# A work list reordered: three more query/key tiles transposed by DMA instead of on TensorE, and zero matmuls at the head

## The chip, the cores and the metric

The kernel runs on one core of a Trainium2 chip. The time is that of one execution in microseconds (us) of device time; lower is better. Six executions of the kernel before took 180.29 to 180.58 us, with a median of 180.43 us.

## What is computed

Four batches of eight heads attend over 768 positions of 64 numbers each. A query sees the first 8 positions and the last 96 up to itself, with a bias that falls with the distance. The 3072 results of 512 numbers then go through a layer that takes the maximum of three matrix products, and through an output product.

```python
scores = scale * np.matmul(q, k.transpose(0, 1, 3, 2))
is_global = pos[None, :] < int(n_global)           # 8
is_local = (rel >= 0) & (rel < int(n_local))       # 96
scores = np.where(is_global | is_local, scores - slope * dist, -1e9)
a = softmax(scores); x = np.matmul(a, v)           # -> (3072, 512)
h = np.maximum(np.maximum(x @ w1, x @ w2), x @ w3) # 512 -> 768
out = h @ w_out                                    # 768 -> 512
```

## The kernel before

**Tiles.** The 3072 tokens are 24 tiles T of 128; six tiles make a batch, and T % 6 == 0 is a batch's first. The tiles are grouped into seven chunks c for the output layers: tiles 0-3, 4-5, 6-7, 8-11, 12-15, 16-19, 20-23. All work is cut into units, and the string `SCHEDULE` names every unit in the order in which it is issued. There is no planner at run time: each engine runs its own instructions in exactly the order in which the string issues them, and waits in that order. One waiting instruction holds up all that stand behind it on its engine. SP is the queue that starts all loads, all stores but one, and the DMA transposes.

**Units of attention.** `l`, `L` and `v` load. `c` and `C` cast to bf16; the last digit of a unit picks the engine (0 ACT, 1 DVE, 2 POOL, 3 split). Tiles 0-11 come in parts (`l`, `c`, and `x`, which transposes on PE). Tiles 12-23, the "single" tiles, are loaded by `L`, cast by `C T.0`, and transposed by `X` (`u_X`): with the digit 4 by a DMA transpose on SP (L250), else by eight PE transposes into PSUM (L261) and copies to SBUF by ACT and/or DVE (L263-L266). `S T.g` computes the scores of four heads into the PSUM slot `sp0` or `sp1` (L283; with the digit 1 the bias is added first by two matmuls, L275), and ACT takes the exponential (L288). `M` multiplies by the mask on DVE (L307). `A` multiplies by the values (L322, L325), into one of the same two PSUM slots, and DVE normalizes (L331, L332). `T` transposes the result: digit 4 by DMA on SP (L340), else by four PE transposes and a copy (L349, L350). `G` and `V` put the 8 global keys and values into place: `G T` after the scores of T and before those of T+1, `V T` after `A T` and before `A T+1`.

**Units of the output layers.** `F c.f.j` is one of the three products (j) for one of six slices (f) of a chunk: four matmuls into a PSUM tile of the pool `psH`, emptied by ACT for j = 0 (L366) and by DVE for j = 1, 2 (L368, L370). They are 512 columns wide, but 256 for the chunks 1 and 2. `O c.t` is the output product of one tile: six matmuls of 512 columns (L376), a copy (L382), a store (L383). `E` is the last chunk's output. `w`, `o`, `W`, `Q` load and cast the weights.

**Rings.** `psH` has three PSUM tiles, shared by F, O, some of the transposes and the zero matmuls. `psT` has one. `sp0` and `sp1` are one tile each. The output staging ring has four tiles. A DMA's completion semaphore is one of eight, so a DMA is issued only when the one eight before it has landed.

**Zero matmuls.** `u_D(i, n)` issues n matmuls of the tile `zeros` on itself (L436); nothing reads the result.

Of the kernel before, what the change touches and what calls it, by code (L numbers as in the profile page):

```python
# [22 lines left out]


SCHEDULE = """
    K0 K1 K2 K3 K4 K5 l1.0 l1.1 D0.3 c0.0.2 B0.1 B1.1 B2.1 B3.0 K6 B4.1 B5.1 c0.1.1 c1.0.2 x0.0.4 B6.1
    B7.1 x0.1.4 S0.0.1 v0 l2.0 l2.1 K7 S0.1.1 G0.0 S1.0.1 S1.1.0 x1.0.3 c1.1.2 M0.0 M0.1 M1.0 v1 x1.1.4
    C0.1.2 v2 A0.1 G1.2 S2.0.1 M1.1 c2.0.2 x2.0.1 C1.1.1 S2.1.0 G2.2 S3.0.1 M2.0 M2.1 C2.1.1 T0.1 S3.1.1
    M3.0 M3.1 c2.1.2 v3 A1.0 C3.1.0 w0.0 V1.2 x2.1.2 w1.0 A2.1 V2.2 A3.0 T1.0 T2.1 T3.1 W1.0.1 W0.0.0
    G3.2 S4.0.0 S4.1.0 F0.0.0 F0.1.0 M4.0 F0.2.0 F0.3.0 G4.1 S5.0.0 M4.1 S5.1.0 w0.1 W0.1.1 w0.2 W0.2.2  # L30
    V3.2 F0.0.1 F0.1.1 F0.0.2 F0.1.2 v4 C4.1.0 A4.0 V4.2 w1.1 W1.1.2 W2.0.0 F0.4.0 F0.5.0 M5.0 M5.1 w1.2
    W1.2.2 v5 W2.1.0 T4.0 F0.2.1 F0.3.1 l3.0 l3.2 F0.4.1 l3.1 c3.0.2 c3.2.2 F0.5.1 o2 C5.1.0 A5.1 l3.3
    F0.2.2 Q2.2 F0.3.2 W2.2.0 o0 T5.0 F0.4.2 o1 F0.5.2 x3.0.0 F1.0.0 F1.1.0 c3.1.1 F1.2.0 x3.2.0 Q0.2
    F1.0.1 F1.1.1 F1.2.1 l4.0 l4.1 c3.3.0 F1.0.2 F1.1.2 F1.2.2 x3.1.2 x3.3.1 F1.3.0 F1.4.0 Q1.2 F1.3.1
    S6.0.0 S6.1.0 v6 v7 v8 G6.0 F1.3.2 F1.5.0 v9 c4.0.1 F1.4.1 S7.0.0 S7.1.0 G7.2 v10 M6.0 M6.1 M7.0
    M7.1 O0.0.0 F1.4.2 c4.1.1 C6.1.2 C7.1.2 L12 F1.5.1 S8.0.0 S8.1.0 x4.0.0 O0.1.0 A6.0 x4.1.2 A7.1 V7.2
    F1.5.2 v11 T6.0 O0.2.0 T7.1 G8.2 C8.1.2 S9.0.0 S9.1.0 G9.1 v12 v13 O0.3.0 F2.0.0 F2.1.0 S10.0.0 M8.0
    M8.1 M9.0 M9.1 S10.1.0 C9.1.2 L13 L14 F2.0.1 F2.1.1 F2.0.2 A8.0 C12.0.1 F2.1.2 G10.2 O1.0.0 V8.2
    A9.1 X12.1 M10.0 M10.1 C10.1.0 C11.1.0 F2.2.0 S11.0.0 S11.1.0 M11.0 M11.1 L15 F2.3.0 F2.4.0 O1.1.0
    V9.2 A10.1 F2.2.1 V10.2 T8.0 F2.3.1 F2.5.0 T9.0 A11.1 F2.4.1 T10.0 F2.2.2 F2.3.2 T11.1 F2.4.2  # L40
    S12.0.0 S12.1.0 F2.5.1 C13.0.2 C14.0.2 C15.0.1 X13.4 F3.0.0 F3.1.0 F3.0.1 G12.1 C12.1.0 F3.2.0
    F3.1.1 F3.2.1 S13.0.0 S13.1.0 F2.5.2 v14 C13.1.0 C14.1.2 M12.0 M12.1 F3.0.2 F3.1.2 X14.4 F3.2.2
    X15.4 G13.2 M13.0 M13.1 S14.0.0 S14.1.0 F3.3.0 F3.4.0 F3.5.0 M14.0 M14.1 G14.1 A12.0 A13.1 F3.3.1
    F3.4.1 F3.5.1 S15.0.0 M15.0 S15.1.0 G15.0 v15 V13.2 L16 L17 v16 T12.4 v17 M15.1 O2.0.0 C15.1.0 A14.0
    V14.2 F3.3.2 F3.4.2 T13.4 F3.5.2 C16.1.0 C16.0.2 X16.3 T14.4 C17.0.2 A15.1 X17.4 O2.1.0 S16.0.0
    S16.1.0 G16.1 L18 V15.2 L19 T15.1 M16.0 O3.0.0 M16.1 F4.0.0 F4.1.0 F4.0.1 F4.1.1 C18.0.2 L20 C19.0.2
    A16.1 F4.2.0 F4.3.0 S17.0.0 S17.1.0 F4.2.1 F4.0.2 F4.3.1 v18 M17.0 v19 M17.1 X18.3 X19.4 C20.0.0
    V16.2 F4.1.2 C17.1.2 O3.1.1 A17.1 F4.2.2 F4.3.2 S18.0.0 M18.0 S18.1.0 M18.1 F4.4.0 T16.4 T17.4
    F4.4.1 C18.1.2 C19.1.1 F4.4.2 X20.4 G18.1 S19.0.0 S19.1.0 F4.5.0 L21 M19.0 M19.1 v20 F4.5.1 A18.0
    T18.4 F4.5.2 A19.1 T19.4 V19.1 C21.0.1 X21.4 G19.1 L22 C22.0.2 L23 X22.4 O3.2.1 O3.3.0 O4.0.1  # L50
    S20.0.0 S20.1.0 M20.0 G20.0 O4.1.0 F5.0.0 F5.1.0 F5.2.0 S21.0.0 S21.1.0 G21.2 F5.0.1 F5.1.1 M20.1
    M21.0 F5.3.0 F5.0.2 F5.1.2 F5.2.1 F5.2.2 v21 C20.1.1 C21.1.2 F5.4.0 S22.0.0 M21.1 S22.1.0 C23.0.0
    F5.3.1 M22.0 M22.1 F5.5.0 F5.3.2 A20.0 V20.2 G22.2 v22 F5.4.1 X23.4 v23 F5.5.1 T20.4 A21.1 V21.1
    T21.4 F5.4.2 F5.5.2 S23.0.0 S23.1.0 M23.0 O4.2.0 M23.1 C22.1.2 A22.0 C23.1.0 O4.3.0 V22.2 T22.4
    A23.1 T23.4 O5.0.1 O5.1.0 O5.2.1 O5.3.0 F6.0.0 F6.1.0 F6.0.1 F6.0.2 F6.2.0 F6.3.0 F6.4.0 F6.1.1
    F6.2.1 F6.1.2 F6.3.1 F6.4.1 F6.2.2 F6.3.2 F6.5.0 F6.4.2 F6.5.1 F6.5.2 E
"""


# [450 lines left out]
```

The softmax here doesn't subtract the row's maximum and nothing guards it: scores larger than these inputs give would overflow.

## Time and profile before

| | |
|---|---|
| median of six executions | 180.43 us |
| the profiled execution | 180.08 us |
| its span, first to last instruction | 178.3 us |
| PE busy (matmul) | 166.4 us, 93% of the span |
| DVE, ACT, POOL busy | 119.2, 103.2, 37.3 us |
| first output-layer matmul (F0.0.0) starts | 23.14 us |
| last copy starts | 175.30 us |

Times inside the execution count from the start of the span. A profile line gives the line of the kernel, the engine, the operation, the output tile, the input tiles and the shape; then the number of instructions, the busy time, the mean time of one, and what ended the idle time before them. PE matmuls are pipelined, so that the time of one (0.38 us for 512 columns) is longer than the slot it takes in a row of them (0.216 us). The chain of waits shows slots.

### The profile page before, as it was taken

The page shows a single profiled execution, that of the slowest core. Times are in us where ns is not written, and L with a number is a line of the kernel's source. Part 1 is how long each engine was busy: PE and PEld are TensorE (multiplying, and loading weights), DVE is VectorE, ACT ScalarE, POOL GpSimd, SP SyncE. Part 2 cuts the span into 40 slices and gives each one's busy share as a digit, 9 for nine tenths or more (in the row PEclk, how much of TensorE's full clock was granted, in tenths as well). Part 3 has the DMA queues.
Part 4 walks back from the last instruction along what each step waited for, and adds up shares of the span by engine and source line. Part 5 has one row for each costly group of instructions (what it writes and reads, how often), then busy time and mean ns, then how long its engine had stood idle before and what let it go on. Part 6 is the DMA issues. An engine that isn't in the chain of part 4 may idle for free.

```text
span 178.3 us, 3963 instructions
## 1 busy us (share of the span) xinstructions
PE 166.4 (93%) x1529; PEld 95.5 (54%) x1551; DVE 119.2 (67%) x237; ACT 103.2 (58%) x160; POOL 37.3 (21%) x65
## 2 busy tenths in 40 slices
PE   3598799999999999999999999999999999999991
PEld 0454645458866677845555555554454555444451
DVE  4629875977796789748978448878357986137610
ACT  4867898737689958555753836351862543440131
POOL 4255203544243012210006024000020401000000
PEclk9999999999999999999999999999999999999999
DMA  5999999999998999799444999669989664700015
GB/s 142 290 271 242 356 321 380 320 360 358 255 204 222 222 250 243 136 206 228 84 90 124 177 252 230 131 123 206 181 158 298 126 129 147 253 12 4 0 46 191
DMA packets 83587, 35.52 MB, mean 199 GB/s; under 512 B 66160, under 2 KB 78320, under 8 KB 83568
## 3 DMA queue, kind: packets, MB, share of 16 engines
q1 hardware_dynamic: 83424, 35.20, 83.3%
q8 instruction: 12, 0.20, 0.5%
q14 instruction: 7, 0.06, 0.1%
q10 hardware_dynamic: 144, 0.07, 0.1%
HBM read 25.17 MB, written 6.29 MB: 176 GB/s over the span
## 4 chain that ended last, share of the span: by engine, by line
PE 83%; SPq 7%; DMA 5%; issue 1%; ACT 1%; DVE 1%; POOL 0%; ACTq 0%
PE h L361 53%; PE po L376 16%; PE sp L283 6%; SPq L158 4%; DMA rawv<-in_v_dram 4%; PE op L322 3%; SPq L174 3%; PE op L325 2%; PE tpp L239 2%; PE xtp L349 2%; DMA out_dram<-ost 1%; ACT ost L382 1%; PE tp L261 1%; DVE xb L332 0%; ACT va L189 0%
## 5 line engine op out<-in xcount | busy, mean ns | idle before, releaser
L361 PE MATMUL h<-xT,w 128*128 128x512 bf16 (+1 forms) x491 | 99.2, 348 | 0.7 <-issue 0.2
L361 PEld LDWEIGHTS <-w 128*128 128x128 bf16 x504 | 47.0, 98 | 40.4 <-DVE w L427 0.3
L288 ACT ACTIVATE P<-sp 128x1024 bf16<-128x1024 f32 (+1 forms) x48 | 43.5, 955 | 20.3 <-PE sp L283 20.0
L368 DVE TENSOR_TENSOR h<-h,h 128x512 bf16<-128x512 bf16 (+1 forms) x42 | 25.3, 609 | 25.6 <-PE h L361 16.3
L366 ACT CAST h<-h 128x512 bf16<-128x512 f32 (+1 forms) x42 | 21.5, 532 | 21.5 <-PE h L361 21.3
L376 PE MATMUL po<-wo,ht 128*128 128x512 bf16 (+2 forms) x147 | 33.1, 362 | 0.5
L370 DVE TENSOR_TENSOR ht<-h,h 128x512 bf16<-128x512 bf16 (+1 forms) x42 | 25.0, 606 | 3.7 <-PE h L361 3.0
L307 DVE TENSOR_TENSOR P<-P,wmask 128x1024 bf16<-128x1024 bf16 x36 | 24.8, 716 | 3.6 <-ACT P L288 3.5
L382 ACT COPY ost<-po 128x512 f32<-128x512 f32 (+2 forms) x20 | 11.2, 564 | 18.4 <-PE po L376 11.2
L376 PEld LDWEIGHTS <-ht 128*128 128x128 bf16 x156 | 14.0, 98 | 13.9
L332 DVE TENSOR_TENSOR xb<-op,rz 128x512 bf16<-128x512 f32 x24 | 16.6, 691 | 0.8
L283 PEld LDWEIGHTS <-qkT 64*128 64x128 bf16 x352 | 10.2, 96 | 9.7 <-issue 8.0
L283 PE MATMUL sp<-qkT 64*128 64x128 bf16 x352 | 15.2, 223 | 0.0
L322 PEld LDWEIGHTS <-P 128*128 128x128 bf16 x192 | 12.5, 97 | 3.0 <-ACT P L288 0.7
L221 POOL COPY va<-vaf 8x260 int32<-8x260 int32 x14 | 6.3, 449 | 34.7 <-PE op L325 34.7
L198 POOL CAST qkb<-raw 128x1024 bf16<-128x1024 f32 x7 | 7.2, 1035 | 27.7 <-DMA raw<-in_k_dram 27.6
L322 PE MATMUL op<-va,P 128*128 128x65 bf16 x160 | 12.4, 193 | 0.5 <-ACT va L189 0.4
L239 PE MATMUL tpp<-identb,qkp 128*128 128x128 bf16 x96 | 7.9, 235 | 4.0 <-POOL qkp L183 3.5
L325 PEld LDWEIGHTS <-P 128*128 128x128 bf16 x160 | 10.5, 97 | 2.0 <-issue 0.4
L325 PE MATMUL op<-va,P 128*128 128x65 bf16 x128 | 9.9, 193 | 0.0
L243 ACT COPY qkT<-tpp 128x1024 bf16<-128x1024 bf16 (+1 forms) x9 | 7.9, 874 | 3.4 <-PE tpp L239 3.4
L239 PEld LDWEIGHTS <-qkp 128*128 128x128 bf16 x96 | 6.4, 106 | 5.8 <-POOL qkp L183 4.4
(66 smaller groups left out, 107.5 us busy)
## 6 DMA issues: line engine op xcount, KB each, us to landing
rawv<-in_v_dram SPq DMA_DIRECT2D x24, 256.0 KB, 5.0
out_dram<-ost SPq DMA_DIRECT2D x23, 256.0 KB, 2.3
rawp<-in_q_dram SPq DMA_DIRECT2D x6, 512.0 KB, 7.3
rawp<-in_k_dram SPq DMA_DIRECT2D x6, 512.0 KB, 7.5
wst<-in_moe_w_dram SPq DMA_DIRECT2D x3, 1024.0 KB, 9.9
raw<-in_q_dram SPq DMA_DIRECT2D x12, 256.0 KB, 4.3
raw<-in_k_dram SPq DMA_DIRECT2D x12, 256.0 KB, 4.8
wst<-in_moe_w_dram SPq DMA_DIRECT2D x3, 512.0 KB, 8.8
```

Of the source, the lines that this page charges most:

```text
L239: nc.tensor.transpose(tp[:, e, j - lo], qb["p", n, s][:, e, 2 * j:2 * j + 2].rearrange("i h d -> i (h d)"), identb)
L283: nc.tensor.matmul(sp[:, hh, j2, ds], qT(T - ds, 1)[hsl, jp], qT(T, 0)[hsl, jp], start=not how, stop=True, skip_group_check=True)
L288: nc.scalar.activation(P[:, :, 0:n], sp.rearrange("p a b d n -> p (a b) d n")[:, :, 0:n], AF.Exp, bias=0.0, scale=scale)
L307: nc.vector.tensor_mul(P, P, wmask[:, g, :, 0:2])
L322: nc.tensor.matmul(o, P[:, i, 0], heads(va[T])[:, h], start=True, stop=(t == 0), skip_group_check=True)
L325: nc.tensor.matmul(o, P[:, i, 1], heads(va[T - 1])[:, h], start=False, stop=True, skip_group_check=True)
L332: nc.vector.tensor_tensor(out=x.rearrange("p (g h) d -> p g h d", g=2), in0=o4[:, :, :, 0:64], in1=rz[:, :, :, None].to_broadcast([128, 2, ...
L361: nc.tensor.matmul(ps, w123[f // 2][:, dm, j, (f % 2) * 128:(f % 2) * 128 + 128], xT[c][:, dm], start=(dm == 0), stop=(dm == 3))
L366: nc.scalar.copy(h01, ps)
L368: nc.vector.tensor_max(h01s[c, f], h01s[c, f], ps)
L370: nc.vector.tensor_max(ht[c][:, f], h01s[c, f], ps)
L376: nc.tensor.matmul(po, ht[c][:, f, tt * 128:(tt + 1) * 128], wo[:, f, cols], start=(f == 0), stop=(f == NF - 1))
```

## The change

The same units are issued in another order, many with another engine digit, and the zero matmuls differ:

- `X`: before, 9 of the 12 single tiles are transposed by DMA, and X12, X16 and X18 on PE. After, all 12 by DMA.
- `T`: 11 by DMA and 13 on PE in both. T8 goes to DMA, T13 to PE.
- `D`: one unit of 3 matmuls of 512 columns before. After, 42 at the head, 12 behind the first transposes and 9 behind the first result, of 128 columns each.
- The value loads v1 and v2 are issued before the second parts of the loads of tiles 4 and 5; the three 512 KB loads of the first weight slices stand together, ahead of the first 1 MB one; the loads of the later tiles stand ahead of more of the output weights. The first weight slices are cast by POOL.
- The engine digits of `c`, `C`, `G`, `V`, `A`, `W`, `O` are dealt anew, some `V` to ACT. The six score units with a bias matmul are the same six.
- The pairs `S T.0 S T.1` are often in the other order or have other units between them; the order of the F units within a chunk is mixed.

The code differs in one line besides the string. The diff, cut:

```diff
 SCHEDULE = """
-    K0 K1 K2 K3 K4 K5 l1.0 l1.1 D0.3 c0.0.2 B0.1 B1.1 B2.1 B3.0 K6 B4.1 B5.1 c0.1.1 c1.0.2 x0.0.4 B6.1
-    B7.1 x0.1.4 S0.0.1 v0 l2.0 l2.1 K7 S0.1.1 G0.0 S1.0.1 S1.1.0 x1.0.3 c1.1.2 M0.0 M0.1 M1.0 v1 x1.1.4
-    C0.1.2 v2 A0.1 G1.2 S2.0.1 M1.1 c2.0.2 x2.0.1 C1.1.1 S2.1.0 G2.2 S3.0.1 M2.0 M2.1 C2.1.1 T0.1 S3.1.1
-    M3.0 M3.1 c2.1.2 v3 A1.0 C3.1.0 w0.0 V1.2 x2.1.2 w1.0 A2.1 V2.2 A3.0 T1.0 T2.1 T3.1 W1.0.1 W0.0.0
-    G3.2 S4.0.0 S4.1.0 F0.0.0 F0.1.0 M4.0 F0.2.0 F0.3.0 G4.1 S5.0.0 M4.1 S5.1.0 w0.1 W0.1.1 w0.2 W0.2.2
...
-    A9.1 X12.1 M10.0 M10.1 C10.1.0 C11.1.0 F2.2.0 S11.0.0 S11.1.0 M11.0 M11.1 L15 F2.3.0 F2.4.0 O1.1.0
...
-    V14.2 F3.3.2 F3.4.2 T13.4 F3.5.2 C16.1.0 C16.0.2 X16.3 T14.4 C17.0.2 A15.1 X17.4 O2.1.0 S16.0.0
...
-    A16.1 F4.2.0 F4.3.0 S17.0.0 S17.1.0 F4.2.1 F4.0.2 F4.3.1 v18 M17.0 v19 M17.1 X18.3 X19.4 C20.0.0
...
-    A23.1 T23.4 O5.0.1 O5.1.0 O5.2.1 O5.3.0 F6.0.0 F6.1.0 F6.0.1 F6.0.2 F6.2.0 F6.3.0 F6.4.0 F6.1.1
+    D2.42 K2 c0.0.0 B3.0 B0.1 B4.1 B2.1 B7.1 B1.1 l1.0 B5.1 B6.1 x0.0.2 K4 c0.1.1 D1.12 K5 x0.1.4 K6
+    S0.0.1 S0.1.1 M0.1 l1.1 S1.0.1 c1.0.1 S1.1.0 K7 c1.1.1 x1.1.4 x1.0.3 M1.0 G0.2 G1.2 v0 C0.1.2 A0.1
+    S2.0.1 M2.0 v1 M1.1 D0.9 S2.1.0 G2.1 S3.0.1 M2.1 C1.1.2 A1.1 V1.0 l2.0 c2.0.2 x2.0.2 K1 v2 C2.1.2
+    A2.0 V2.1 M0.0 l2.1 c2.1.2 v3 w0.0 W0.0.2 S3.1.1 T0.0 C3.1.1 G3.0 M3.0 x2.1.4 A3.0 T1.0 S4.1.0 T2.1
+    T3.1 M3.1 K3 S4.0.0 w0.1 W0.1.2 M4.1 F0.0.0 F0.1.0 F0.1.1 K0 M4.0 w0.2 G4.2 W0.2.2 F0.0.1 w1.0
...
+    T5.0 c3.2.0 F0.5.2 F0.2.2 F1.0.0 F1.5.0 l3.0 c3.0.0 x3.2.0 F1.0.1 F1.0.2 F1.4.0 F1.5.1 F1.5.2 x3.0.0
+    l3.3 F1.2.0 l3.1 c3.3.2 x3.3.2 c3.1.1 x3.1.3 S7.0.0 F0.3.2 M7.0 F1.1.0 S7.1.0 S6.0.0 G6.1 G7.0
+    F1.1.1 F1.1.2 F1.3.0 F1.3.1 l4.0 c4.0.2 v6 C6.1.1 F1.3.2 S6.1.0 M6.1 o0 S8.0.0 o2 v9 C9.1.2 o1
+    x4.0.2 M6.0 F1.4.1 F1.2.1 S8.1.0 A6.0 F1.2.2 Q0.0 F1.4.2 M7.1 F0.4.2 l4.1 Q2.2 c4.1.1 G8.2 S9.0.0
...
+    O1.1.0 T7.1 M8.1 v11 S10.1.0 L14 C8.1.1 S10.0.0 L15 C13.0.2 O0.2.0 C12.0.2 X12.4 M10.1 F2.0.0 F2.5.0
+    A8.0 V8.0 F2.3.0 F2.0.1 F2.3.1 T8.4 A9.0 M10.0 O1.0.1 V9.1 G10.0 F2.3.2 C11.1.1 S11.1.0 M11.1
...
+    M20.0 S20.1.0 F5.5.0 M20.1 F5.5.1 F5.4.0 A20.0 F5.3.0 F5.5.2 G20.2 S21.1.0 M21.1 S21.0.0 G21.1 V20.0
+    F5.4.1 M21.0 F5.3.1 X22.4 S22.1.0 v21 C21.1.2 S22.0.0 M22.1 v23 v22 O4.2.0 A21.1 F5.4.2 V21.2 G22.2
+    S23.0.0 M22.0 S23.1.0 T20.4 T21.4 F5.1.2 C22.1.2 F5.3.2 A22.0 V22.2 M23.1 C23.1.2 O5.0.0 T22.4 M23.0
+    O4.1.0 A23.0 T23.4 O5.2.0 O5.1.1 O5.3.0 F6.0.0 F6.0.1 F6.3.0 F6.2.0 F6.4.0 F6.2.1 F6.2.2 F6.4.1
...
 """
@@ -433,7 +433,7 @@
         wp = psH.tile([128, 512], FP32, name="wp", tag="h")
         for _ in range(n):
-            nc.tensor.matmul(wp, zeros[:, 0:128], zeros, start=True, stop=True)
+            nc.tensor.matmul(wp[:, 0:128], zeros[:, 0:128], zeros[:, 0:128], start=True, stop=True)
```

More of the change, by code (lines that the diff above doesn't have):

```diff
@@ L31 @@
[L31 to L35, printed above, removed]
@@ L36 @@
-    M7.1 O0.0.0 F1.4.2 c4.1.1 C6.1.2 C7.1.2 L12 F1.5.1 S8.0.0 S8.1.0 x4.0.0 O0.1.0 A6.0 x4.1.2 A7.1 V7.2
-    F1.5.2 v11 T6.0 O0.2.0 T7.1 G8.2 C8.1.2 S9.0.0 S9.1.0 G9.1 v12 v13 O0.3.0 F2.0.0 F2.1.0 S10.0.0 M8.0
-    M8.1 M9.0 M9.1 S10.1.0 C9.1.2 L13 L14 F2.0.1 F2.1.1 F2.0.2 A8.0 C12.0.1 F2.1.2 G10.2 O1.0.0 V8.2
-    A9.1 X12.1 M10.0 M10.1 C10.1.0 C11.1.0 F2.2.0 S11.0.0 S11.1.0 M11.0 M11.1 L15 F2.3.0 F2.4.0 O1.1.0
-    V9.2 A10.1 F2.2.1 V10.2 T8.0 F2.3.1 F2.5.0 T9.0 A11.1 F2.4.1 T10.0 F2.2.2 F2.3.2 T11.1 F2.4.2
@@ L41 @@
[L41 to L44, printed above, removed]
-    V14.2 F3.3.2 F3.4.2 T13.4 F3.5.2 C16.1.0 C16.0.2 X16.3 T14.4 C17.0.2 A15.1 X17.4 O2.1.0 S16.0.0
@@ L46 @@
-    S16.1.0 G16.1 L18 V15.2 L19 T15.1 M16.0 O3.0.0 M16.1 F4.0.0 F4.1.0 F4.0.1 F4.1.1 C18.0.2 L20 C19.0.2
-    A16.1 F4.2.0 F4.3.0 S17.0.0 S17.1.0 F4.2.1 F4.0.2 F4.3.1 v18 M17.0 v19 M17.1 X18.3 X19.4 C20.0.0
-    V16.2 F4.1.2 C17.1.2 O3.1.1 A17.1 F4.2.2 F4.3.2 S18.0.0 M18.0 S18.1.0 M18.1 F4.4.0 T16.4 T17.4
-    F4.4.1 C18.1.2 C19.1.1 F4.4.2 X20.4 G18.1 S19.0.0 S19.1.0 F4.5.0 L21 M19.0 M19.1 v20 F4.5.1 A18.0
-    T18.4 F4.5.2 A19.1 T19.4 V19.1 C21.0.1 X21.4 G19.1 L22 C22.0.2 L23 X22.4 O3.2.1 O3.3.0 O4.0.1
@@ L51 @@
[L51 to L54, printed above, removed]
-    A23.1 T23.4 O5.0.1 O5.1.0 O5.2.1 O5.3.0 F6.0.0 F6.1.0 F6.0.1 F6.0.2 F6.2.0 F6.3.0 F6.4.0 F6.1.1
@@ L56 @@
-    F6.2.1 F6.1.2 F6.3.1 F6.4.1 F6.2.2 F6.3.2 F6.5.0 F6.4.2 F6.5.1 F6.5.2 E
+    D2.42 K2 c0.0.0 B3.0 B0.1 B4.1 B2.1 B7.1 B1.1 l1.0 B5.1 B6.1 x0.0.2 K4 c0.1.1 D1.12 K5 x0.1.4 K6
[3 more added lines that the diff above has]
+    T3.1 M3.1 K3 S4.0.0 w0.1 W0.1.2 M4.1 F0.0.0 F0.1.0 F0.1.1 K0 M4.0 w0.2 G4.2 W0.2.2 F0.0.1 w1.0
@@ new lines @@
+    W2.0.0 V3.2 W1.0.1 F0.1.2 F0.0.2 S5.1.0 M5.1 v4 C4.1.2 S5.0.0 F0.3.0 F0.5.0 w1.1 W1.1.0 W2.1.1
+    F0.4.0 v5 M5.0 C5.1.0 F0.2.0 A4.0 V4.2 F0.4.1 F0.2.1 A5.1 T4.0 w1.2 F0.3.1 W2.2.0 W1.2.0 F0.5.1 l3.2
+    T5.0 c3.2.0 F0.5.2 F0.2.2 F1.0.0 F1.5.0 l3.0 c3.0.0 x3.2.0 F1.0.1 F1.0.2 F1.4.0 F1.5.1 F1.5.2 x3.0.0
+    l3.3 F1.2.0 l3.1 c3.3.2 x3.3.2 c3.1.1 x3.1.3 S7.0.0 F0.3.2 M7.0 F1.1.0 S7.1.0 S6.0.0 G6.1 G7.0
+    F1.1.1 F1.1.2 F1.3.0 F1.3.1 l4.0 c4.0.2 v6 C6.1.1 F1.3.2 S6.1.0 M6.1 o0 S8.0.0 o2 v9 C9.1.2 o1
@@ new lines @@
+    x4.0.2 M6.0 F1.4.1 F1.2.1 S8.1.0 A6.0 F1.2.2 Q0.0 F1.4.2 M7.1 F0.4.2 l4.1 Q2.2 c4.1.1 G8.2 S9.0.0
+    S9.1.0 G9.0 v7 C7.1.1 v8 L12 L13 v10 Q1.2 O0.1.0 M9.0 O0.3.0 A7.1 V7.1 x4.1.2 C10.1.2 T6.1 M9.1 M8.0
+    O1.1.0 T7.1 M8.1 v11 S10.1.0 L14 C8.1.1 S10.0.0 L15 C13.0.2 O0.2.0 C12.0.2 X12.4 M10.1 F2.0.0 F2.5.0
+    A8.0 V8.0 F2.3.0 F2.0.1 F2.3.1 T8.4 A9.0 M10.0 O1.0.1 V9.1 G10.0 F2.3.2 C11.1.1 S11.1.0 M11.1
+    S11.0.0 M11.0 O0.0.0 T9.0 v13 F2.4.0 A10.1 V10.2 F2.1.0 X13.4 C14.0.3 X14.4 v16 v12 F2.1.1 F2.1.2
@@ new lines @@
+    v14 A11.0 F2.2.0 T10.0 v15 F2.0.2 F2.5.1 F2.2.1 F2.2.2 T11.0 G12.2 F2.4.1 F2.5.2 F2.4.2 L16 S12.1.0
+    S12.0.0 C15.0.2 X15.4 M12.0 F3.0.0 F3.3.0 F3.0.1 F3.0.2 F3.4.0 F3.3.1 S13.0.0 M13.0 S13.1.0 G13.2
+    M12.1 L18 F3.4.1 F3.4.2 F3.2.0 M13.1 L17 S14.1.0 C13.1.0 S14.0.0 G14.0 F3.3.2 F3.1.0 F3.5.0 C12.1.1
+    A12.0 C15.1.0 M14.1 C16.0.2 X16.4 F3.5.1 A13.1 V13.2 F3.2.1 F3.1.1 C14.1.0 M14.0 F3.1.2 S15.0.0
+    S15.1.0 F3.2.2 F3.5.2 C18.0.2 A14.0 T12.4 T14.4 V14.0 X18.4 C17.0.0 L19 C19.0.2 C16.1.0 M15.1 v18
@@ new lines @@
+    X17.4 O2.0.0 M15.0 T13.1 O3.1.0 X19.4 v17 A15.0 V15.2 v19 O3.0.0 G15.1 T15.0 S16.1.0 S16.0.0 G16.1
+    O2.1.1 M16.0 M16.1 L20 F4.0.0 F4.2.0 F4.4.0 S18.1.0 S18.0.0 F4.2.1 F4.2.2 A16.1 V16.1 F4.3.0 F4.0.1
+    F4.0.2 M18.0 S17.0.0 S17.1.0 F4.3.1 M17.1 F4.3.2 T16.4 M18.1 M17.0 L21 S19.0.0 M19.0 S19.1.0 M19.1
+    C18.1.2 O3.3.1 F4.4.1 C17.1.2 G18.2 F4.5.0 A17.0 A18.1 T17.4 F4.5.1 C20.0.0 T18.4 O3.2.1 G19.1
+    F4.1.0 C19.1.2 A19.1 V19.0 T19.4 F4.1.1 F4.4.2 X20.4 F4.1.2 L23 L22 v20 F4.5.2 O4.0.0 C21.0.1 X21.4
@@ new lines @@
+    C22.0.2 O4.3.0 F5.0.0 F5.2.0 F5.2.1 F5.0.1 F5.2.2 C23.0.0 X23.4 F5.0.2 F5.1.0 F5.1.1 C20.1.2 S20.0.0
+    M20.0 S20.1.0 F5.5.0 M20.1 F5.5.1 F5.4.0 A20.0 F5.3.0 F5.5.2 G20.2 S21.1.0 M21.1 S21.0.0 G21.1 V20.0
+    F5.4.1 M21.0 F5.3.1 X22.4 S22.1.0 v21 C21.1.2 S22.0.0 M22.1 v23 v22 O4.2.0 A21.1 F5.4.2 V21.2 G22.2
+    S23.0.0 M22.0 S23.1.0 T20.4 T21.4 F5.1.2 C22.1.2 F5.3.2 A22.0 V22.2 M23.1 C23.1.2 O5.0.0 T22.4 M23.0
+    O4.1.0 A23.0 T23.4 O5.2.0 O5.1.1 O5.3.0 F6.0.0 F6.0.1 F6.3.0 F6.2.0 F6.4.0 F6.2.1 F6.2.2 F6.4.1
@@ L57 @@
+    F6.4.2 F6.5.0 F6.1.0 F6.5.1 F6.3.1 F6.0.2 F6.1.1 F6.3.2 F6.1.2 F6.5.2 E
 """
```

## The prediction

> **What bounds the kernel now.** I read the busy table first, then what PE waited for, then the chain of waits for the price of each kind of unit.
>
> ```profile
> PE 166.4 (93%) x1529; PEld 95.5 (54%) x1551; DVE 119.2 (67%) x237; ACT 103.2 (58%) x160; POOL 37.3 (21%) x65
> ```
>
> Matmuls fill 93% of the span. Whether that is a full engine or a stretched one is told by the list of PE's waits, taken from 25 us to the end:
>
> ```profile
> PE h L361 <- issue: 0.2, 1, 0.2
> ```
>
> That is all: from the first output-layer matmul at 23.14 us to PE's last at 174.7 us it waits for nobody. The chain gives the slots:
>
> ```profile
> 65.74 0.45 PE tp L261 x8
> 66.19 0.44 PE h L361 x4
> 66.63 0.55 PE sp L283 x16
> ...
> 95.72 0.22 PE tp L261 x4
> 95.94 0.22 PE tpk L261 x4
> ...
> 109.03 0.22 PE tp L261 x4
> 109.26 0.22 PE tpk L261 x4
> ```
>
> Eight transposes hold PE for 0.45, a 256-wide F for 0.44, two score units for 0.55 (0.65 with the change-over: matmuls end at 26.56, the scores start at 26.65, the next F at 27.20). In the same way a 512-wide F holds it 0.86, an O 1.30, an A 0.48, a T 0.22. So the time is the start of F0.0.0, plus PE work, plus PE stalls (now none), plus a tail that is not touched. The start is set here:
>
> ```profile
> 19.81 0.63 ACT va L189
> ...
> 21.44 0.70 DVE xb L332
> 22.14 0.05 issue
> 22.19 0.40 PE xtp L349 x4
> 22.59 0.55 PE sp L283 x16
> 23.14 0.34 PE h L361
> ```
>
> The last of tile 3's values is cast at 20.44, A3 and its normalization end at 22.13, T3 at 23.05. Two rows of the timeline show something that the granted-clock row (full throughout) does not:
>
> ```profile
> 10.24 1.04 PE L275 MATMUL sp<-bias,identb 128*128 128x512 bf16 x2
> 14.13 0.59 PE L275 MATMUL sp<-bias,identb 128*128 128x512 bf16 x2
> ```
>
> The same two matmuls take 0.43 apiece at 10 us and 0.21 at 14 us (0.17 of drain taken off): PE runs at half speed until about 12 us.
>
> [...]
>
> **Removed from PE.** X12, X16 and X18 lose their eight transposes: 0.45 + 0.44 + 0.45 = **-1.34**. All of it lies where PE waits for nothing, so all of it is on the path. Their copies leave ACT and DVE too (0.58 and 0.42, 0.68 for X12), which are off the path. In their place come DMA transposes:
>
> ```profile
> qkT<-qkb SPq DMA_TRANSPOSE x9, 3.2
> ```
>
> They land in 3.1 to 4.5 us and hold the issuing queue 1.2 to 2.3 us. X12 is now issued 36 units ahead of S12, with some 12 us of PE work between; for X16 and X18 there are over 7 us at the row's worst. Behind them on SP stand T8, the stores and loads. Stores have a ring of four; before, SP already stood until 133.0 for X22 with four results waiting, and PE did not stop. I cost them at nothing; without that cover it would be the 4.5 us of a landing less what PE has in hand.
>
> **PE change-overs.** After F0.0.0 the score units form 20 groups where they formed 19, at 0.10 each: **+0.10**. T8 and T13 swap sides: nothing.
>
> **The head.** The zero matmuls need no data. Three of 512 columns took 1.46 us cold, 0.43 a slot, so 42 of 128 take a quarter each: 4.5 us, from 1.2 to 5.7. At worst they go at the 0.12 of the cold transposes (8 in 1.03): to 6.2. The first cast ends at 6.1 in either order (5.03 and 1.05 on ACT, as on POOL), so 0 to 0.1. The 12 behind the first transposes fill a wait for a cast.
>
> The later path, at the warm speed: tile 2-3's keys land at 10.44 in both; cast 0.69, PE 0.45 and 0.2 of drain and semaphores, two DVE copies 0.6 and 1.22, to 13.8. S2 0.33 and 0.2, then three exponentials of 1.03, which overlap 0.1 (the third waits for its PSUM slot 0.1), to 17.7. V1 is now on ACT, where the trace has no such copy: 0.22 by its smallest copy, 0.63 by its cast of a whole tile; 0.3 as DVE and POOL take 0.27 and 0.39. A2 0.48 and 0.2, to 18.65; S3.1 with its bias 0.75 and the drain, exponential, to 20.5; A3 0.65, DVE 0.2 and 0.69, T3 0.4 and 0.42: F0.0.0 at **23.15**, against 23.14. v3 is behind the same bytes as before (landed 19.78) and its cast on DVE ends by 20.2, ahead of the 20.5. The head brings **0**, from -0.3 (V1 at 0.22 and no wait) to +0.4 (V1 at 0.63, zeros in the way).
>
> The half speed matters here, since 4.2 us of PE work (44 transposes and zero matmuls, the bias and scores of tiles 0-3) stand between 6.1 and 13 us. I take full speed from about 6 us: 4.5 us of unbroken matmuls precede it, where before it took 6 us of broken ones from 6.12.
>
> [...]
>
> **New stalls.** The new order leaves less between a PE write and the reuse of its PSUM tile.
>
> ```profile
> L288 ACT ACTIVATE P<-sp 128x1024 bf16<-128x1024 f32 x40 | 39.0, 1027 | 15.1 <-PE sp L283 14.8
> L288 ACT ACTIVATE P<-sp 128x512 bf16<-128x512 f32 x8 | 4.4, 594 | 5.2 <-PE sp L283 5.2
> L243 ACT COPY qkT<-tpp 128x1024 bf16<-128x1024 bf16 x6 | 6.1, 1020 | 2.7 <-PE tpp L239 2.7
> ```
>
> - Before F1.2.2 (about 51 us): it takes the `psH` tile of x4.0, which ACT copies after the exponentials of S6.1 and S8.0. From the end of S6.1 on PE, ACT needs 0.2 + 0.59 + 1.03 + 1.02 - 0.2 = 2.64 and a semaphore 0.05. PE has S8.0 0.33, x4.0 0.45, F1.4.1 and F1.2.1 0.44 each, S8.1 0.33, A6 0.26 = 2.25. **+0.45**. Queued behind F1.2.2 is all of PE.
> - Before S6.0 (46 us): `sp0` is free after ACT has done x3.0, F1.2.0, x3.3 and S7.0's exponential, 0.67 + 1.02 + 0.39 + 1.02 + 1.03 - 0.3 = 3.83 against 3.73 of PE work: **+0.10**.
> - Before S22.1 (140 us): G21 stands on DVE behind M21.1, which waits for the exponential of S21.1. 0.2 + 1.03 + 0.69 + 0.17 against S21.0 0.33 and two F 1.73: **+0.05**.
> - Slack under 0.3 at F2.2.2, A15, F4.5.1, A20, A23, and F6.0.0, where three O (3.9) must cover A23 to T23's landing (0.2 + 0.95 + 2.45 and semaphores, 3.7). Lower bound 0; upper 1.3 if each DVE row there costs its whole time where rows overlap by 0.08 now. I take **+0.10**, near the lower end, as PE has not one such wait now.
>
> **Sum.** -1.34 + 0.10 + 0 + 0.45 + 0.10 + 0.05 + 0.10 = **-0.54**. The profiled execution, 180.08, would be 179.54; it lies 0.35 under the median, so the median goes from 180.43 to **179.9 us**. What this kernel can tell from no change is 0.2%, 0.36 us.
>
> **Rivals.**
> - *The whole 1.34 is kept*: the stalls above vanish (ACT's overlap is larger than the rows show) and the head gives 0.1: 179.1. For it: no PE wait now. Against: ACT is in order and its rows agree within 0.01.
> - *Hidden or given back* (the change does not do what it says): the tight places cost 0.5 instead of 0.10, and PE's gain is gone: 180.4. For it: six places within 0.3. Against: none of them waits by the rows.
> - *Slower: the clock comes late.* If PE stays at half speed until 12 us as before, the 4.2 us of work there take up to 8.4; 2.4 us of waits hide part, and I take 1.0 as what reaches A0 and everything after: 180.9, up to 181.3. Without a late clock there is no loss here; it decides from a release later than about 9.5 us. For it: there are breaks of 0.3 to 1 us after the zeros, and a 0.4 us break from 7.15 did not speed it up before. Against: before, PE was idle from 2.65 to 6.12.
>
> **How the numbers follow.** Forecast 0.50 (own range 179.5 to 180.3, by the bounds of the head and the tight places), whole gain 0.12, given back 0.17, late clock 0.21. The range, 179.0 to 181.2, takes in the whole gain and most of the late clock. Faster (under 180.07): 0.40 of the forecast and the whole gain, 0.52. Same: 0.10 of the forecast and 0.15 of the third, 0.25. Slower: the rest of the third and the late clock, 0.23.
>
> **What would show it.** Right: no L261 row, twelve L250 transposes, F0.0.0 at 23.1, a PE wait of about 0.45 for the L243 copy near 51 us and hardly another after it, PE's last matmul 0.5 earlier; the bias pair of S1 at 0.6, not 1.04. Wrong: F0.0.0 at 24 with slow transposes at 8 to 12 us (late clock); several PE waits on DVE after 70 us; PE waiting for `qkT` or `xT`, which would mean that SP's queue is the bound.

## The result, and the profile after

The changed kernel takes **181.13 us** (median of 15 executions, 180.29 to 181.62), the kernel before 180.46 (33 executions, 180.27 to 180.67). The ratio is 1.0037, with a 95% interval of 1.0028 to 1.0045: slower by 0.37%, where 179.9 and a small gain were forecast. Measured again beside its variants it took 181.30 (1.0044, interval 1.0026 to 1.0062). Of the 0.67 about half lies within the span (medians 179.0 and 178.7) and half beyond it (2.12 and 1.78).

The profiled execution took 181.49, one of the longer ones, with a span of 179.4. The first part of its page, and the row of DMA transposes:

```profile
PE 169.1 (94%) x1565; PEld 98.2 (55%) x1587; DVE 121.2 (68%) x235; ACT 107.1 (60%) x165; POOL 33.6 (19%) x58
...
qkT<-qkb SPq DMA_TRANSPOSE x12, 3.9
```

All twelve X go by DMA, land in 3.9 us (3.1 to 5.8), and no PE wait names them. But PE is no longer dense. What it waited for from 23 us on (engine, tile and line, what it waited for, us in total, times, longest):

```profile
PE op L322 <- DVE xb L332: 0.3, 1, 0.3
PE h L361 <- DVE ost L382: 0.3, 1, 0.3
PE h L361 <- DVE xT L350: 0.3, 1, 0.3
PE h L361 <- issue: 0.2, 1, 0.2
```

The last is the one line that the kernel before has too; the third is the wait of F0.0.0 itself, at the start; the first two are new. And these are only the waits before a matmul; those before a weight load stand apart. The whole of it comes out by the slots: between the ends of two F's, take off the slots of the units in between, and what is left is waiting. By this measure the kernel before has none. The chain of waits, which in the kernel before runs through PE from F0.0.0 to the last F, but for one piece of 0.36 on POOL, now goes through DVE (start, us, engine, tile, line):

```profile
61.30 1.18 DVE va L189
62.48 1.44 DVE P L307
...
114.03 2.23 DVE P L307 x3
```

The changed kernel was profiled three times. Of the second time it was expected:

> The changed kernel once more, unchanged, for a second profile. If the collisions of DVE and POOL depend on the moment at which loads land (POOL's casts wait for loads, DVE's work for PE), the stretched masks and casts are in part others, and the span differs by the sum of PE's waits; if the waits are a matter of the order alone, they are the same eight at the same places to 0.05.

The sums, against the profile of before (180.08). The end of an F is taken here, and in the experiments, at the end of its last weight load:

| us | forecast | profile 181.49 | profile 180.27 |
|---|---|---|---|
| end of F0.0.0 (before: 23.63) | 0 | +0.27 | +0.10 |
| PE work, F0.0.0 to the last F, by the slots | -1.24 | -1.13 | -1.13 |
| PE waits in the same stretch | +0.70 | +1.98 | +0.93 |
| last F to the end of the span (before: 9.33) | 0 | -0.05 | -0.04 |
| beyond the span, the time less the span (before: 1.77) | 0 | +0.34 | +0.34 |
| sum | -0.54 | +1.41 | +0.19 |

So the work was taken off nearly as forecast (0.11 less), and two things took it back: waits that differ from execution to execution of the same program, and a third of a microsecond beyond the span. Where the waits lie:

| place | forecast | 181.49 | 180.27 | third profile (181.81) |
|---|---|---|---|---|
| 43 to 47 us, x3.0, S7.0, S6.0 | 0.10 | 0.13 | 0.13 | 0.95 |
| 51 us, A6.0 and F1.2.2 | 0.45 | 0.10 | 0.39 | 0.13 |
| 63 and 66 us, A8.0 and A9.0 | 0 | 0.68 | 0 | 0.59 |
| 117 us, F4.5.1 | in 0.10 | 0.46 | 0.19 | 0.19 |
| 142 us, S22.1 | 0.05 | 0.32 | 0 | 0 |
| 155 us, F6.0.0 | in 0.10 | 0.22 | 0.21 | 0.21 |

**What the waits are.** DVE's timeline at 62 us in the profile of 181.49 (start, us, engine, line, operation, tiles, shapes, count):

```profile
61.23 1.26 DVE L189 CAST va<-rawv 128x512 bf16<-128x512 f32 x1
62.40 1.52 DVE L307 TENSOR_TENSOR P<-P,wmask 128x1024 bf16<-128x1024 bf16 x1
63.84 0.20 DVE L331 RECIPROCAL rz<-op 128x8 f32<-128x8 f32 x1
```

The cast C8.1 takes 0.42 elsewhere, the mask M10.1 0.68. Beside them POOL casts C13.0 and C12.0, back to back:

```profile
60.71 2.67 POOL L198 CAST qkb<-raw 128x1024 bf16<-128x1024 f32 x2
```

POOL's second cast ends at 63.38, and M10.1 0.54 later, at 63.92. That fits a mask of 0.68 which stands still until POOL is about done, and whose recorded 1.52 contain the standing. In the execution of 180.27 the same instructions met otherwise, because the load of v10, for which POOL waited, landed 1.3 us later (POOL's cast of it starts at 61.46 instead of 60.15):

```profile
61.11 0.41 DVE L189 CAST va<-rawv 128x512 bf16<-128x512 f32 x1
61.45 0.67 DVE L307 TENSOR_TENSOR P<-P,wmask 128x1024 bf16<-128x1024 bf16 x1
```

```profile
61.46 1.14 POOL L189 CAST va<-rawv 128x512 bf16<-128x512 f32 x1 [8.87 <-DMA rawv<-in_v_dram]
```

Here DVE started first, by 0.01 us, and took its 0.67, and POOL's cast of 0.62 took 1.14. In these rows the one that starts first takes its own time, and the other longer, as if it stood still. Both executions are of one program, so the order on DVE is not what differs. At 43.5 us it is the same with a cast of each; in the profile of 181.49 DVE starts first (43.54, 0.69) and POOL's cast at 43.99 takes 1.14 instead of 1.04; in the third profile POOL is first by 0.08, and DVE's cast takes twice its time, on which x3.1 on PE waits 0.7:

```profile
43.67 1.50 DVE L183 CAST qkp<-rawp 128x1024 bf16<-128x1024 f32 x1
```

```profile
43.59 1.04 POOL L183 CAST qkp<-rawp 128x1024 bf16<-128x1024 f32 x1 [2.25 <-DMA rawp<-in_q_dram]
```

DVE's maxima (L368, L370), which read one input from PSUM, are spared in the profiles of 180.08 and 181.49: those of 128x512 take 0.67 to 0.69 beside POOL's casts (14 in the kernel before, 9 in the changed kernel), as they do elsewhere. Three of them in the kernel before, with POOL beside them:

```profile
94.55 1.89 DVE L370 TENSOR_TENSOR ht<-h,h 128x512 bf16<-128x512 bf16 x3
```

```profile
94.00 2.02 POOL L198 CAST qkb<-raw 128x1024 bf16<-128x1024 f32 x2
```

The other two places in the profile of 181.49. DVE at 114 and 141 us, and POOL beside it:

```profile
113.95 2.31 DVE L307 TENSOR_TENSOR P<-P,wmask 128x1024 bf16<-128x1024 bf16 x3
...
141.09 0.59 DVE L216 COPY qkT<-kg 128x32 bf16<-128x32 bf16 x1
```

```profile
114.23 0.89 POOL L189 CAST va<-rawv 128x512 bf16<-128x512 f32 x1
...
140.66 0.99 POOL L189 CAST va<-rawv 128x512 bf16<-128x512 f32 x1 [6.33 <-DMA rawv<-in_v_dram]
```

The second of the three masks at 114 us takes 1.09 instead of 0.68, the copy of O3.3 stands behind them on DVE, and F4.5.1 on PE waits for that copy's PSUM tile. At 141 us G21, a copy of 0.17, takes 0.59, and S22.1 waits for it.

F6.0.0's 0.22 is another matter. SP's own rows:

```profile
150.26 1.23 SPq L340 DMA_TRANSPOSE xT<-xb  x1
151.59 0.53 SPq L383 DMA_DIRECT2D out_dram<-ost  x1
152.22 1.23 SPq L340 DMA_TRANSPOSE xT<-xb  x1
```

A23's result is ready at 151.92, but T23's transpose stands behind the store of O4.1, which stood behind T22: 0.30 late.

### The profile page after: what moved, and what is told of

Read it like the earlier page. It is cut to its first block, busy times and chain, and to the rows that moved or that the text cites. A ratio compares the mean times of both kernels' runs of the same rounds, so it can differ in the third digit from the quotient of the medians.

```text
span 179.4 us, 4018 instructions
## 1 busy us (share of the span) xinstructions
PE 169.1 (94%) x1565; PEld 98.2 (55%) x1587; DVE 121.2 (68%) x235; ACT 107.1 (60%) x165; POOL 33.6 (19%) x58
## 4 chain that ended last, share of the span: by engine, by line
PE 70%; SPq 10%; DVE 7%; DMA 7%; ACT 3%; issue 2%; ACTq 0%
PE h L361 45%; PE po L376 14%; DMA wst<-in_moe_w_dram 5%; PE sp L283 5%; SPq L174 4%; SPq L158 4%; DVE P L307 3%; PE op L322 3%; PE op L325 2%; ACT P L288 2%; SPq L417 2%; PE tpp L239 1%; DMA out_dram<-ost 1%; PE xtp L349 1%; DVE xb L332 1%
## 5 line engine op out<-in xcount | busy, mean ns | idle before, releaser
L368 DVE TENSOR_TENSOR h<-h,h 128x512 bf16<-128x512 bf16 (+1 forms) x42 | 25.2, 607 | 23.1 <-PE h L361 21.5
L307 DVE TENSOR_TENSOR P<-P,wmask 128x1024 bf16<-128x1024 bf16 x36 | 27.1, 767 | 3.2 <-ACT P L288 2.9
L370 DVE TENSOR_TENSOR ht<-h,h 128x512 bf16<-128x512 bf16 (+1 forms) x42 | 25.4, 609 | 5.1 <-PE h L361 3.6
L198 POOL CAST qkb<-raw 128x1024 bf16<-128x1024 f32 x7 | 7.9, 1132 | 34.8 <-DMA raw<-in_k_dram 34.8
L189 POOL CAST va<-rawv 128x512 bf16<-128x512 f32 x11 | 7.5, 684 | 28.6 <-DMA rawv<-in_v_dram 24.5
L243 ACT COPY qkT<-tpp 128x1024 bf16<-128x1024 bf16 (+1 forms) x10 | 8.9, 886 | 1.4 <-PE tpp L239 1.4
L382 DVE COPY ost<-po 128x512 f32<-128x512 f32 (+1 forms) x6 | 3.7, 619 | 7.5 <-PE po L376 7.5
L331 DVE RECIPROCAL rz<-op 128x8 f32<-128x8 f32 x24 | 4.9, 203 | 4.6 <-PE op L325 3.4
```

What stands on the lines that cost most here:

```text
L307: nc.vector.tensor_mul(P, P, wmask[:, g, :, 0:2])
L368: nc.vector.tensor_max(h01s[c, f], h01s[c, f], ps)
L370: nc.vector.tensor_max(ht[c][:, f], h01s[c, f], ps)
L382: copy(ost, po)
```

## The experiments

The kernels of experiments 1, 3 and 7, and the one with 42 zeros in 8, have one line less than the others: in their rows the line numbers are one lower for the same code.

**1. X by DMA alone, in the kernel before.**

```diff
-    ... A9.1 X12.1 M10.0 ...
+    ... A9.1 X12.4 M10.0 ...
-    ... M15.1 O2.0.0 C15.1.0 ... C16.1.0 C16.0.2 X16.3 T14.4 ...
+    ... C16.0.2 X16.4 M15.1 O2.0.0 C15.1.0 ... C16.1.0 T14.4 ...
-    ... L20 C19.0.2 ... M17.1 X18.3 X19.4 ...
+    ... L20 X18.4 C19.0.2 ... M17.1 X19.4 ...
```

> The kernel before with X12, X16 and X18 as DMA transposes (X16 and X18 issued somewhat earlier on SP), nothing else changed. If PE work is the time, 24 transposes less are worth 1.34; X12's 0.45 was also cover for the normalization of A9, on whose slot S11.1 waits, so up to 0.4 of it comes back: 0.9 to 1.3 below the kernel before, 179.1 to 179.5. If the DMA transposes cost elsewhere (SP's queue, late landings), the time stays at 180.2 or above.

Measured: 179.94, ratio 0.9973 (0.9964 to 0.9983): 0.49 gained, not 0.9. From the end of F0.0.0 to the end of the last F, PE takes 144.45 instead of 145.35: -0.89, that is 1.34 less the wait of S11.1, which is 0.45 by the slots and stands in the list of waits as

```profile
PE sp L282 <- DVE xb L331: 0.3, 1, 0.3
```

Another 0.46 is lost behind PE: from the last F's end to the end of the span it takes 9.79 instead of 9.33, though the last store is issued 0.37 earlier than before. Experiment 9 comes back to this.

**2. The cover for S11.1, with and without a longer run of zeros at the head.**

```diff
-    ... F2.2.0 S11.0.0 S11.1.0 M11.0 M11.1 L15 F2.3.0 ... V9.2 A10.1 ...
+    ... F2.2.0 F2.3.0 S11.0.0 S11.1.0 M11.0 M11.1 L15 ... V9.2 A10.0 ...
```

on top of experiment 1; the first of the two also has `D2.11` for `D0.3` in the place of the three zero matmuls (11 of 512 columns).

> The kernel before with X12, X16, X18 by DMA (as in the first run), F2.3.0 moved ahead of S11.0 and A10 in the slot sp0, so that S11.1's wait of 0.45 has work in front of it, and 11 zero matmuls of 512 columns at the head. PE work theory: the whole 1.34 less nothing, against the first run (179.94) another 0.45 off: 179.4 to 179.6. If the slots only hand the wait on to A10 or S12: 179.9.

> The kernel before with the three X by DMA and the cover for S11.1, with the three zero matmuls of 512 columns it had. If the zeros bring nothing (with 11 of them alone 180.54 against 180.43): 179.3 to 179.5, as with them. If they are worth something once PE's work is less: 179.7 or more.

Measured: 179.41 (0.9948, interval 0.9935 to 0.9961) with 11 zeros, 179.60 (0.9950, interval 0.9938 to 0.9962) with three. PE takes 144.01 us in both: -1.34, the whole of the forecast. After the start of F0.0.0 the list of PE's waits is empty again (with three zeros). On PE, three X by DMA are worth their slots; 0.30 to 0.43 of that is lost behind the last F (experiment 9). The zeros bring nothing that the intervals can tell.

**3. POOL's casts moved away from DVE's work, first try.**

```diff
-    ... L15 C13.0.2 O0.2.0 C12.0.2 X12.4 M10.1 ... V10.2 F2.1.0 X13.4 C14.0.3 ...
+    ... L15 O0.2.0 M10.1 ... V10.2 C13.0.2 C12.0.2 X12.4 F2.1.0 X13.4 C14.0.3 ...
-    ... C17.1.2 G18.2 F4.5.0 ... F4.1.0 C19.1.2 A19.1 ...   S21.0.0 G21.1 V20.0
+    ... C17.1.2 G18.2 C19.1.0 F4.5.0 ... F4.1.0 A19.1 ...   S21.0.0 G21.2 V20.0
```

> The changed kernel with POOL's work taken from beside DVE's at three places: the casts C13.0 and C12.0 stand behind V10 on POOL (X12 with them), C19.1 goes to ACT, G21 from DVE to POOL. Theory 'DVE and POOL shut each other out': the mask M10.1 takes 0.68 instead of 1.52, the cast C8.1 0.42 instead of 1.26, the masks at 114 us 0.68 each, and the waits of PE at A8, A9, F4.5.1 and S22.1 (0.20, 0.48, 0.46, 0.32 in the profile of the changed kernel) go: 1.2 to 1.5 off, 179.6 to 180.0. Rival 'order alone' (the instructions ahead of A8's normalization and of the copy of O3.3 on DVE are simply too many): these stand there as before, only G21's wait goes: 0.3 off, 180.8.

Measured: 181.82 (1.0081, interval 1.0069 to 1.0093), slower still. The four waits are gone: by the slots nothing is lost at 63 to 66, 117 and 142 us. C8.1 and M10.1 are issued in the same order on DVE as in the changed kernel, and now run undisturbed:

```profile
61.35 0.41 DVE L188 CAST va<-rawv 128x512 bf16<-128x512 f32 x1
61.69 0.67 DVE L306 TENSOR_TENSOR P<-P,wmask 128x1024 bf16<-128x1024 bf16 x1
```

But the casts now run at 70 us, beside DVE's half of C14.0. DVE and POOL there, and PE's wait:

```profile
70.81 2.41 DVE L194 CAST qkb<-raw 128x512 bf16<-128x512 f32 x1
```

```profile
70.36 2.02 POOL L197 CAST qkb<-raw 128x1024 bf16<-128x1024 f32 x2
72.34 0.60 POOL L195 CAST qkb<-raw 128x512 bf16<-128x512 f32 x1
```

```profile
PE h L360 <- DVE h L367: 1.2, 1, 1.2
```

A cast of 128x512, which takes 0.41 undisturbed, took 2.41, to 73.22, 0.28 after the last of POOL's three (72.94): as if it stood through all of them. PE lost 1.75 there. The time was missed, the mechanism shown more plainly than planned: the same POOL casts, moved, free one place and block another. As DVE's order at 62 us is unchanged, it is not that order which made them slow; experiment 4, where DVE's work moves, could not tell.

**4. Second try: DVE's side moved.** C13.0 and C12.0 stay; C8.1 goes to ACT, M10.1 behind A9's normalization, C19.1 and G21 as in 3.

```diff
-    ... M8.0 O1.1.0 ... L14 C8.1.1 S10.0.0 ... X12.4 M10.1 F2.0.0 ... A9.0 M10.0
+    ... M8.0 C8.1.0 O1.1.0 ... L14 S10.0.0 ... X12.4 F2.0.0 ... A9.0 M10.1 M10.0
```

> The changed kernel with POOL and DVE kept apart otherwise: POOL's casts C13.0 and C12.0 stay in place, but the cast C8.1 goes from DVE to ACT (before O1.1) and the mask M10.1 stands behind A9's normalization; C19.1 on ACT and G21 on POOL as in the run before. Theory 'shut out': nothing of DVE that PE waits for runs beside a POOL cast at 60 to 64, 114 and 141 us, and no new pair is made at 70 us: PE's waits at A8, A9, F4.5.1, S22.1 go, 1.2 to 1.5 off, 179.6 to 180.0. If other causes hold these places, 180.8 or more.

> The changed kernel itself, unchanged, side by side with the two below. If its median of 181.13 holds here too, the single mends took off 0.45 to 0.70 each; if it is at 180.3 to 180.7 here, as the one execution of 180.27 suggests, the collisions of 62, 114 and 141 us are rarer than in the profile of 181.49, and the mends bring 0.3 or less.

> The kernel with all three places mended (as in the run with C8.1 on ACT and M10.1 moved, median 179.99), beside the changed kernel. If the collisions cost the changed kernel what its first profile shows, its span is 0.8 to 1.2 below that of the changed kernel here; if they are rare, 0.2 to 0.5.

Measured: 179.99 (0.9984, interval 0.9965 to 1.0002, which does not tell it from the kernel before), and measured a second time, beside the changed kernel at 181.30, 180.23 (0.9989, interval 0.9981 to 0.9998). The median span falls from 179.15 to 178.5, by 0.65 (0.8 in the first measurement, against the changed kernel's 15 executions): between the two expectations, which fits collisions that are there in part of the executions. Side by side, the spans of the changed kernel spread over 2.0 (178.3 to 180.3), those of the mended one over 1.0 (178.0 to 179.0); in the first measurement one of its executions came to 180.0 all the same. In the later profile PE waits 0.44 in all after F0.0.0, 0.2 of it at F6.0.0; in the earlier one 1.0, of which 0.47 at 50 us. Nearly all of the rest of the 1.07 (0.34) lies beyond the span (experiment 6).

**5. The three places one by one.** C8.1 and M10.1 alone; C19.1 alone; G21 alone.

> The changed kernel with one of the three places mended: the cast C8.1 on ACT and the mask M10.1 behind A9's normalization. In the two profiles of the changed kernel the waits of PE at A8 and A9 were 0.20 and 0.48, and 0 and 0.06. Theory 'shut out': no wait there in any execution, 0.1 to 0.6 off the median 181.13. If the place is free by chance in most executions anyway, no change (181.0 to 181.3).

> The changed kernel with the cast C19.1 on ACT instead of POOL, nothing else. F4.5.1's wait (0.46 and 0.19 in the two profiles) falls to under 0.2; 0.1 to 0.3 off the median 181.13. Rival (order on DVE alone): no change.

> The changed kernel with G21 on POOL instead of DVE, nothing else. S22.1's wait (0.32 and 0 in the two profiles) is gone in every execution; 0 to 0.3 off the median 181.13.

Measured: 180.43 (1.0008), 180.68 (1.0010), 180.55 (1.0013), each with an interval of about 0.0011 to 0.0015 to either side. The profiles show the waits of the mended place gone, and those of the others as chance has them. By the median span the three are 0.3, 0.45 and 0.45 below the changed kernel's 179.0, more than the expectation for the last two, and the sum (1.2) is more than all three mended at once (0.8). With spans that spread over 1 to 1.5 us, what one place is worth is not settled to better than 0.3.

**6. Two instructions less on DVE.** The part beyond the span is 2.07 to 2.19 in all executions of the changed kernel, and 1.72 to 1.85 in the kernel before's variants. Beside it, the number of DVE's rows in the trace, those that only wait among them: 311 in the changed kernel and in two variants (2.1), 310 with G21 moved (2.00), 308 or 309 in others (1.75 to 1.78). But it is 1.8 again with 322 to 329 in the rest, so it is not simply the more rows the longer. To take three rows off, two copies go to ACT:

```diff
-    ... G16.1 O2.1.1 ... T18.4 O3.2.1 ...
+    ... G16.1 O2.1.0 ... T18.4 O3.2.0 ...
```

> The changed kernel with two instructions less on DVE: the copies of O2.1 and O3.2 go to ACT. Executions of the changed kernel take 2.1 us beyond their span, all others but two 1.75 to 1.8; those with 2.0 to 2.1 have 310 or 311 instructions on DVE in the trace, the others 309 or less, or 322 and more. If DVE's program length is the cause, the part beyond the span falls to 1.75 to 1.80 and the time by 0.33, while the span moves by 0.2 at most. If it comes from something else in the order, it stays at 2.1.

Measured: 180.88 beside 181.30. The part beyond the span is 1.78 (1.74 to 1.82) instead of 2.12, the median span 179.1 against 179.15. So two copies fewer on DVE take 0.34 of the loss away, with no change in the span. What happens beyond the span no trace shows, and why it is so stays open.

**7. The changed kernel without its zeros** (`D0.3`, now of 128 columns, for `D2.42`; no `D1.12`, no `D0.9`).

> The changed kernel without its zero matmuls, but for three of 128 columns at the head. If the zeros bring the clock early and PE's speed is on the head's path: half speed until about 12 us, F0.0.0 0.5 to 1.0 later, 181.6 to 182.1. If ACT and DVE set the head: F0.0.0 within 0.2 of the 23.34 it has with zeros, time 181.0 to 181.3, though the bias pair of S1 takes 1.04 instead of 0.59.

Measured: 182.30 (1.0106, interval 1.0088 to 1.0124): the clock, told by the speed of the matmul rows, is on the head's path of this order. The bias pair of S1 and sixteen transposes behind it, then rows of the changed kernel:

```profile
10.75 1.04 PE L274 MATMUL sp<-bias,identb 128*128 128x512 bf16 x2
...
12.68 1.89 PE L238 MATMUL tpp<-identb,qkp 128*128 128x128 bf16 x16
```

```profile
6.07 1.01 PE L239 MATMUL tpp<-identb,qkp 128*128 128x128 bf16 x8 [0.22 <-ACT qkp L183]
6.89 0.85 PE L436 MATMUL wp<-zeros 128*128 128x128 bf16 x12
...
10.47 0.59 PE L275 MATMUL sp<-bias,identb 128*128 128x512 bf16 x2
```

With the drain of 0.17 off, eight transposes at 6.07 take 0.105 each, twelve zeros at 6.89 take 0.057: with the zeros full speed begins near 6.9 us in this profile. Without them sixteen transposes at 12.68 still take 0.108 each. In the 13 profiles of kernels with zeros it begins, by the same rows, between 4.4 and 7.1 us. F0.0.0 ends at 25.31 instead of 23.90, somewhat more than expected, but this profile is of the slowest of six executions; the median span is 180.2 against 179.0.

**8. Zeros in the kernel before**: 42 of 128 columns, and 11 of 512, as long on PE with a quarter of the instructions.

> The kernel before with 42 zero matmuls of 128 columns at the head in place of three of 512. If the early clock helps by itself: full speed from about 7 us, the bias pair of S1 at 0.59, F0.0.0 up to 0.8 earlier, 179.6. If the landing of v3 (19.78) and its cast hold A3 as before: F0.0.0 within 0.2 of 23.14, 180.2 to 180.5.

> The kernel before with 11 zero matmuls of 512 columns at the head: as long on PE as the 42 of 128 columns (4.7 us at half speed), but with 22 instructions instead of 84. In the run with 42, PE's first code load (16 KB on queue 8, over 1 us on one of the 16 DMA engines) came at 14.5 us instead of 16.3, and v1 and all later loads landed late, the first weights 1.5 to 2 us. Theory 'more instructions bring the code load into the head's loads': it comes at about 16 us again, the second and third weight slices land within 0.5 of the kernel before (25.5 and 27.1), PE has no waits of 0.7 for weights at 26 us, time 180.0 to 180.4. Rival 'unbroken zeros hurt by themselves': 180.7 as with 42.

Measured: 180.72 (1.0018, interval 1.0004 to 1.0033) and 180.54 (1.0013, interval 0.9998 to 1.0028). Both have the bias pair at full speed at 9.7 us, and both wait for v3 as before (landed 19.87 and 20.23, against 19.78): the earlier clock does not bring F0.0.0 forward here. With 42, PE also waits for weights:

```profile
PE h L360 <- DVE w L426: 0.5, 1, 0.5
```

By the slots it loses 1.1 us from 25 to 31 us. The trace has loads of instructions, 16 KB each, on queue 8; that they are PE's is inferred, as the first starts at 13.85 us in the changed kernel and at 14.5 with 42 zeros here, but after 16 us with 11 or three. The stretch from 12 to 16 us in the view of the DMA queues has one with 42 zeros (the line is the same in the changed kernel's view) and none with 11 or in the kernel before, whose first come at 16.8 and 16.25:

```profile
q8 instruction: 1, 0.02, 1.9%
```

The line's 1.9% of 16 engines over 4 us is 1.2 us of one engine. Behind this load transfers land later: v1 at 17.7 (before 16.5), the second and third slices of the first weights at 27.5 and 29.1 (before 25.5 and 27.1; with 11 zeros 25.9 and 27.5). That the load causes it is argued from these times and from the run with 11 zeros; no row names it. The landings were as expected with 11 zeros, the time a little above.

**9. A longer DVE program for the best kernel**, experiment 2 with 11 zeros and four pieces moved from ACT to DVE.

```diff
-    G15.0 ... G20.0 ... O2.1.0 ... O4.1.0
+    G15.1 ... G20.1 ... O2.1.1 ... O4.1.1
```

> The kernel before with X by DMA, the cover and 11 zero matmuls (179.41), and four pieces moved from ACT to DVE (G15, G20, the copies of O2.1 and O4.1), so that DVE's program is as long as in the kernel before (about 326 instructions instead of 322). In the three kernels with 322 or 323 the stretch from the last F's end to the end of the span took 9.65 to 9.74 instead of 9.32, with a last code load on queue 14 at 175 instead of 170.6. If DVE's program length sets that, the load comes at about 170 and the stretch is 9.3 again: 179.0 to 179.15. If not, 179.4, and up to 179.8 if the moved pieces make PE wait.

Measured: **178.98** (0.9930, interval 0.9913 to 0.9947), faster than both kernels. With 329 DVE instructions the last code load on queue 14 starts at 168.6; with 322 it stood in the stretch from 174 us to the end:

```profile
q14 instruction: 1, 0.01, 0.7%
```

From the last F's end to the end of the span it takes 9.26 instead of 9.63. That closes the account of experiments 1 and 2, where this stretch takes 0.46, 0.30 (11 zeros) and 0.43 (three) more than before: -0.89 and 0.46 are -0.43 (measured -0.49); -1.34 and 0.30 are -1.04 (measured -1.01); -1.34 and 0.43 are -0.91 (measured -0.87). That the load is DVE's is argued from the counts alone; its engine is not recorded.

## Why the prediction was wrong

*Removed from PE, -1.34: right.* With no other change it is -1.34 to the hundredth on PE (experiment 2), and the cover by DMA held: no wait names `qkT`. In the changed kernel the slots give -1.13 in place of the forecast -1.24, so the change-overs cost a little more than 0.10. X12 stands 50 units ahead of S12, not 36; the cover was greater than stated (landed at 72.2 us, needed from 76.0).

*Head, 0 with -0.3 to +0.4: inside its bounds* (+0.27 and +0.10). The clock came at 6.9, where about 6 was taken; the rival of the late clock had the right sign for the wrong reason. Experiment 7 shows its price (1.2 us) when it does happen. The measured 181.13 lies in the part of the stated range (179.0 to 181.2) that was put there for this late clock, which did not come; that the range took it in is luck.

*New stalls, +0.70: the step that failed.* Its durations came from undisturbed rows, and DVE and POOL were treated as independent. A mask of 0.68 became 1.52, a cast of 0.42 became 1.26, a copy of 0.17 became 0.59, at places where the new order had left slack of 0 to 0.3. The "tight places" term, 0.10 with an upper end of 1.3, and S22.1's 0.05 (its own figures give 0.03) are the terms mis-sized; in the two profiles the waits came to 1.98 and 0.93 in place of 0.70. The place at 62 us was not named at all, nor was x3.1 at 45 us, which waits 0.7 in the third profile. The kernel before has such collisions too (a mask of 1.03 at 32.3 us, one of 1.10 at 139.7), but none with PE behind it, so the empty wait list hid what they cost.

*F1.2.2, +0.45: wrong premise.* In the built program F1.2.2 waits for DVE, and only F1.4.2 for ACT's copy of x4.0: F1.2.2 starts at 51.86 us, and that copy ends at 52.05. PE waited there 0.10 to 0.39, and in the profile where it was 0.39, 0.3 of it was A6.0 waiting for a mask of DVE that stood beside POOL's cast of the output weights.

*F6.0.0: its slack of under 0.3 was gone*, as T23 on SP stands behind a store.

*Nothing beyond the span: wrong by 0.34*, which goes with DVE's instructions (experiment 6), for a cause that stays open; the prediction had no term for it. *Rivals:* "given back" named the right kind of cause, with 0.5 for the tight places where 0.2 to 1.3 more than forecast was lost.

## What to carry to other kernels

In a kernel whose main engine is dense, work taken off it is worth its slots only while every wait that it covered still has something in front of it (here 0.89 of 1.34 with S11.1 left uncovered, 1.34 with the cover); count the instructions that are left with little slack (0 to 0.3 us here). For those, take DVE's and POOL's times as if they excluded one another (here, beside POOL's casts, a mask of 0.68 took up to 1.52, a cast of 0.41 up to 2.41 and a copy of 0.17 up to 0.59, and the maxima that read PSUM kept their 0.67 to 0.69), and look at which load POOL's instruction waits for: the order in the program does not fix which of the two starts first (at 43.5 us DVE by 0.45 in one execution, POOL by 0.08 in another). After reordering, read two or three profiles, not one, and compare the part beyond the span too.
